# Attention and a squared-ReLU layer in one kernel: first product in pairs of blocks, plainer early blocks, a new written order

## The chip, the cores and the metric

The kernel runs on one core of a Trainium2 chip. The metric is the device time of one execution in microseconds (us). The core has TensorE (PE, matrix products into PSUM), VectorE (DVE), ScalarE (ACT), GpSimd (POOL) and SyncE (SP), each with its own queue of instructions, and DMA engines that POOL and SP feed here.

## The reference

The inputs `q`, `k`, `v` have 4 batches, 8 heads, 768 positions and 64 columns; `w_in` is 512 x 2048 and `w_out` 2048 x 512. All are float32.

```python
scores = q @ k.T / sqrt(64) - slope[h] * dist          # dist: distance back, 96 for the 8 global keys
keep   = (key < 8) | (0 <= query - key < 96)
a      = softmax(where(keep, scores, -1e9))            # over the keys
x      = (a @ v), heads side by side, as 3072 x 512
out    = relu(x @ w_in) ** 2 @ w_out                   # 3072 x 512
```

## The kernel before

**Tiles and blocks.** The 3,072 rows are 24 tiles of 128; tile j = 6b + t is the t-th of batch b. Since a query sees at most 95 keys back and 8 global ones, a tile needs its own keys and those of the tile before it, into which the 8 global ones are copied (`gk` for keys, `gv` for values; every first tile of a batch needs only itself). Two tiles make a block: 12 blocks of 256 rows go through the two layers.

**Attention, per tile.** POOL loads q, k and v with a cast to bf16 (`ld` for the first six tiles, line 330; `load` later, line 334). Queries and keys are transposed: for tiles below `JQK` = 8 by PE through the identity (`tr`, line 528) and a copy out of PSUM (`T`, lines 453 on ACT, 455 on DVE), for the others by one DMA transpose that SP issues (`T`, line 554). `sc` (line 618) makes scores with products of 64 rows. In tiles 0 to 2 the bias, a scaled identity `sid[h]` times a mask, is added by PE ahead of the scores (`bias`, line 597); later tiles multiply the exponential (`exp`, line 684, ACT) by a table `E` (`mul`, line 709, DVE). `pv` (line 767) makes the output and, from a column of ones, the sum, for four heads in a PSUM bank. `norm` (lines 797 and 798, DVE) takes the reciprocal and multiplies, once for each four heads. The tile is transposed again into `xT`: below `JX` = 8 by PE (`trx`, line 835) and a copy, later by DMA (line 859, SP).

**First layer, per block.** In the plain form (`s1`, line 1081) PE makes one step of 256 hidden columns from 8 products of 256 moving columns; `relu` (lines 884, 886) and `sq` (lines 1117, 1119) follow. In the other form (`first_seven`) the block is seen as a 2 x 2 matrix of quarters, here two halves of the 512 input columns and the block's two tiles, and seven products p1 to p7 take the place of eight (line 967). DVE makes sums of `w_in`'s quarters once (`isum`, line 907) and of the block's quarters (`xs`, line 939). The products of one group of steps gather in three PSUM banks, and the order within a group is tied:

```python
p1 = product("p1", "x", (0, 0), (0, 0), True)
u1 = copy(1, "x", p1)
p6 = product("p6", "x", 1, 1, False, [u1])
u2 = copy(2, "x", p6)
p7 = product("p7", "x", 3, 2, False, [u2])
u3 = copy(3, "x", p7)
p4 = product("p4", "x", (1, 1), 3, False, [u3])
```

`u` copies a part result out (453, 455); `c` adds one back and applies the ReLU (line 1011), `q` squares (lines 1031, 1033). Each of these products has 8 matmuls of 128 moving columns, for one tile. Before the change, block 0 and the first half of block 1 are plain; the second half of block 1 (`SEVEN1_PART`) and blocks 2 to 11 (`SEVEN1`) have the seven products.

**Second layer, per block.** All 12 blocks (`SEVEN`) use seven products as well (`s2`, line 1230, matmuls of 256 moving columns), with sums of `w_out` (`wsum`, line 1150) and of the hidden block (`sum`, written to `hsum`, line 1185). `part` and `o` (line 1305) bring the results out, `st` (line 1327) stores through SP.

**What sets the order.** Every step is an operation of a `Plan`. The text constant `ORDER` names all operations in one sequence, with the PSUM banks or buffers that each takes (`:hex digits`) and its engine (`@A` ACT, `@V` DVE). Each engine runs its own operations in that sequence, and semaphores hold it where an operand or a buffer is not ready. POOL and SP follow the sequence too, so a transpose that waits for its load holds the stores behind it. Rings limit how far work can run ahead: 16 buffers, 3 `xT`, 3 hidden blocks (`NHB`), 12 transposed key and query tiles (`NKT`), 10 value tiles (`NV`).

**Head.** Ahead of the planned part, PE runs `NWARM` = 8 products of 512 columns on zeros (line 396), while DVE makes the mask tables, then both identities, then `sid` for the 8 heads (line 414), and ACT fills `E` (line 421).

Of the kernel before, what the change touches and what calls it, by code (L numbers as in the profile page):

```python
# [57 lines left out]
tr.0.0:0 T.0.0@V tr.1.0:1 bias.0.0:23 T.1.0@V ld.q.1 ld.k.1 tr.0.1:4 T.0.1@V ld.q.2 ld.k.2 E0.1 ld.q.3 ld.v.0 ld.k.3  # L58
tr.1.1:5 T.1.1@A ld.v.1 sc.0.0 bias.1.0:6701 exp.0.1.0:0 sc.1.0 tr.0.2:4 exp.0.0.0 gk.1@A T.0.2@V exp.1.0.0:1 tr.1.2:5
T.1.2@V bias.2.0:3264 sc.2.0 exp.1.1.0 exp.1.1.1:3 ld.k.4 exp.1.0.1 ld.q.4 pv.0.1:5 tr.0.3:7 pv.0.0:1 ld.v.2 gk.2@A  # L60
exp.2.1.1:4 exp.2.0.0:5 exp.2.0.1 exp.2.1.0 tr.1.3:0 T.0.3@V T.1.3@V sc.3.0:4730 norm.0.0:0 norm.0.1 pv.1.0:6 tr.1.4:1
ld.q.5 pv.1.1:2 norm.1.0:1 norm.1.1 trx.0:5 exp.3.1.1:6 ld.k.5 gv.1@A ld.v.3 tr.0.4:0 T.1.4@V T.0.4@V xT.0@A:0 gk.3@V
trx.1:6 exp.3.0.1 exp.3.1.0:7 exp.3.0.0 ld.win.1.0 pv.2.0:2 pv.2.1:5 norm.2.0:0 norm.2.1 gv.2@V mul.3.0:8 sc.4.0:1037
exp.4.1.0:9 trx.2:2 ld.win.4.0 xT.1@A exp.4.1.1:a tr.1.5:4 tr.0.5:5 T.1.5@A exp.4.0.0 xT.2@A:1 mul.3.1:b pv.3.0:0
pv.3.1:6 T.0.5@A s1.0.1:7 norm.3.0:1 gk.4@V exp.4.0.1 norm.3.1 gv.3@A s1.0.1#2 trx.3:4 sc.5.0:0126 exp.5.0.1:c
exp.5.1.0:d s1.0.4:5 exp.5.1.1 E0.0 mul.4.0:e xT.3@V ld.v.4 mul.4.1:f ones.6 pv.4.0:3 s1.1.1:4 relu.0.4@V:2 exp.5.0.0
ld.win.3.0 s1.0.3:2 pv.4.1:1 relu.0.1@A:0 sq.0.1@A:0 gv.4@A s1.0.3#2 mul.5.1:1 s1.1.3:6 norm.4.0:0 norm.4.1 ld.win.2.0
# [5 lines left out]
relu.0.6@A:a ld.wout.6 ld.wout.5 ld.wout.4 u.2.1.1@A:e relu.0.7@A:c isum.3.1 s1.0.0#4 h.2.1.p5:4 s1.0.2#3 relu.0.0@A:f
h.1.1.p1:6 h.2.1.p2:7 u.1.1.1@A:0 isum.2.1 h.2.1.p6 u.2.1.2@A:d h.1.1.p2:2 c.1.1.c11:3 xs.2.2 c.2.1.c11:5 sq.0.0@A
s1.0.2#4 isum.2.0 h.1.1.p6 u.1.1.2@A:1 h.2.0.p6 u.2.0.2@A:4 h.2.1.p7 u.2.1.3@A:8 h.1.1.p7 h.2.0.p5:5 relu.0.2@A:6
u.1.1.3@A:2 h.2.0.p7 wsum.0.0 h.1.1.p5:2 u.2.0.3@A:7 c.2.1.c22:b wsum.1.0 sq.0.2@A gate.9 s1.0.5:7 h.2.1.p3 wsum.2.0
c.2.0.c22:f load.6 load.7 c.1.1.c22:0 sq.0.7@A relu.0.5@A:e sq.0.6@A sq.0.5@A load.8 c.2.1.c12:8 sum.0.2:0 sum.0.0
h.1.1.p4 h.2.0.p4 wsum.0.1 s2.1.p1.0:0 T.8 c.2.0.c21@A:6 h.2.0.p3 h.2.1.p4 s2.0.p1.0:7 h.1.1.p3 sum.0.1 s2.0.p2.0:4
q.1.1.c22@A q.1.1.c11@A s2.0.p1.1 q.2.1.c22@A:2 q.2.0.c11@A part.0.p1@A:0 c.1.1.c21@A:c s2.0.p2.1 s2.1.p1.1 wsum.1.1
s2.0.p6.0 s2.0.p6.1 c.1.1.c12:7 tr.1.6:1 tr.0.6:6 part.1.p1@A:1 q.1.1.c21@A s2.1.p2.0:2 q.2.1.c11@A sum.0.3 wsum.2.1  # L80
part.0.p6@A:2 o.0.p2:a c.2.1.c21@A:2 s2.1.p2.1 wsum.3.1 wsum.3.0 T.1.6@V s2.0.p7.0 s2.0.p7.1 gate.12 s2.0.p5.0
q.1.1.c12@A s2.0.p5.1 c.2.0.c12:e load.9 part.0.p7@A:3 q.2.1.c12@A T.0.6@A q.2.0.c22@A o.0.p5:d s2.0.p4.0 s2.0.p4.1
q.2.0.c12@A o.0.p4@A sum.1.0:1 s2.0.p3.0 tr.0.7:3 gate.13 sum.1.1 s2.0.p3.1 o.1.p2:0 o.0.p3 sum.1.2 T.0.7@A tr.1.7:1
sum.2.2:0 sum.1.3 sum.2.0 T.1.7@A q.2.0.c21@A s2.1.p6.0 s2.1.p6.1 q.2.1.c21@A part.1.p6@A:0 sc.6.0:567341 exp.6.1.0:3
load.10 gk.7@A exp.6.0.0 s2.1.p5.0 s2.1.p7.0 s2.1.p7.1 mul.6.0:b exp.7.0.0:9 exp.7.1.0 part.1.p7@A:3 s2.2.p1.0:6
s2.1.p5.1 sum.2.1 exp.7.0.1:1 exp.7.1.1 o.1.p5:c mul.7.0:5 s2.2.p1.1 pv.6.0:5 norm.6.0:0 s2.1.p4.0 s2.1.p4.1 o.1.p4@A
pv.6.1:7 s2.1.p3.0 sc.8.0:3415 exp.8.0.1:7 part.2.p1@A:1 pv.7.0:0 s2.1.p3.1 mul.7.1:8 norm.6.1 T.9 pv.7.1:7 norm.7.0:1
norm.7.1 trx.6:1 exp.8.1.0:4 xT.6@V:0 exp.8.1.1 exp.8.0.0 s2.2.p6.0 s2.2.p6.1 o.1.p3 gate.15 trx.7:0 xT.7@A gk.8@V
# [76 lines left out]
sum.11.1#2 st.8.1 st.9.1 sum.11.2 o.10.p4@A s2.11.p6.0 s2.11.p6.1 st.10.1 o.11.p2:0 st.11.0 sum.11.2#2 part.11.p6@V:1  # L165
s2.10.p3.0 s2.10.p3.1 st.9.0 s2.11.p7.0 s2.11.p7.1 o.10.p3 st.10.0 st.7.1 sum.11.3#2 part.11.p7@V:3 sum.11.3
s2.11.p5.0 s2.11.p5.1 o.11.p5:b s2.11.p4.0 s2.11.p4.1 o.11.p4@V s2.11.p3.0 s2.11.p3.1 st.11.1 st.11.1#2 o.11.p3
st.11.0#2
"""


@with_exitstack
def kernel(
# [743 lines left out]
    def first_seven(blk, groups=(0, 1)):  # L917
# [142 lines left out]
        for g in groups:  # L1060
            group(g)
# [388 lines left out]
```

## Time and profile before

| | |
|---|---|
| median of 3 runs | 197.23 us |
| lowest, highest | 196.97, 197.88 us |
| span of the profiled execution | 195.7 us |
| granted clock of TensorE in it | 1.000 |
| instructions in the span | 6835 |
| DMA | 26.92 MB, mean 138 GB/s |

The profile is of one execution, and the page gives no other time of its own for it than the span, from the first to the last instruction. What the run has beyond that lies around the span. The page lists busy time by engine; a row of the stages gives the busy time of the engines in a stretch; the chain of work that ended last is followed back from the last instruction, each piece to what released it. "PE bank L967" is TensorE writing a PSUM bank at line 967. A matmul's own duration contains the way through the array, so the pace of a row of matmuls is read from a long piece, not from the mean duration of one.

### The profile page before, as it was taken

Reading aid. Unit: us, or ns where it says so; the run is one execution under the profiler, and the core shown is the slowest. Engines: PE = TensorE matmul, PEld = TensorE weight load, DVE = VectorE, ACT = ScalarE, POOL = GpSimd, SP = SyncE. Lnnn points to the kernel's source line nnn. Section 1 sums busy time; section 2 is a strip of 40 time slices with the busy share of each in tenths; the row PEclk is TensorE's granted clock in tenths of the full one; section 3 lists DMA queues with packets and bytes.
Section 4 is the critical chain, followed back from the end, with each engine's and each line's share of the span. In section 5 each row is a group of like instructions: output and inputs, shape, how many; then the busy total and the mean of one; then the engine's idle time right before and its main releaser. Section 6 shows DMA issues by size and latency. Waiting matters only on the chain.

```text
span 195.7 us, 6835 instructions
## 1 busy us (share of the span) xinstructions
PE 188.5 (96%) x2808; PEld 170.5 (87%) x2808; DVE 179.4 (92%) x437; ACT 161.6 (83%) x338; POOL 75.1 (38%) x93
## 2 busy tenths in 40 slices
PE   7986999999999999999999999999999999999993
PEld 3774999999888989989989989989889999999982
DVE  8569989999999999989999999899999899999982
ACT  6699999999989797999899997587987798986600
POOL 8999784775564502650047080119200000000000
PEclk9999999999999999999999999999999999999999
DMA  7999999999999999999949989999947440152026
GB/s 125 149 150 167 179 193 205 205 162 151 155 150 143 99 177 168 119 100 227 139 79 129 138 74 119 209 168 97 147 113 188 85 136 13 20 193 105 0 91 234
DMA packets 111713, 26.92 MB, mean 138 GB/s; under 512 B 103234, under 2 KB 108866, under 8 KB 111682
## 3 DMA queue, kind: packets, MB, share of 16 engines
q0 software_dynamic: 80256, 13.37, 91.9%
q1 hardware_dynamic: 31426, 13.11, 33.4%
q8 instruction: 22, 0.36, 0.7%
q14 instruction: 9, 0.07, 0.1%
HBM read 27.26 MB, written 6.29 MB: 171 GB/s over the span
## 4 chain that ended last, share of the span: by engine, by line
PE 85%; POOL 6%; DMA 5%; DVE 1%; issue 0%; POOLq 0%; DVEq 0%
PE bank L1230 37%; PE bank L967 32%; PE bank L1081 6%; PE bank L618 5%; PE bank L767 5%; POOL qk_first L330 5%; DMA win<-in_moe_w_in_dram 3%; DMA xT<-x 2%; POOL v L330 2%; PE bank L835 1%; PE bank L528 0%; DVE xs L939 0%; DVE buf L886 0%; DVE hsum L1185 0%; DVE early L1305 0%
## 5 line engine op out<-in xcount | busy, mean ns | idle before, releaser
L684 ACT ACTIVATE buf<-bank 128x512 bf16<-128x512 f32 x76 | 41.5, 613 | 2.8 <-PE bank L618 2.7
L1031 ACT ACTIVATE hs<-buf 128x512 bf16<-128x512 f32 x62 | 37.2, 635 | 2.5 <-DVE buf L1011 2.0
L1230 PEld LDWEIGHTS <-hsum 128*128 128x128 bf16 x384 | 35.3, 98 | 4.0
L453 ACT COPY buf<-bank 128x512 f32<-128x512 f32 (+1 forms) x59 | 32.1, 569 | 7.7 <-PE bank L967 6.1
L1230 PE MATMUL bank<-wsum,hsum 128*128 128x256 bf16 x288 | 38.0, 273 | 0.0
L1011 DVE CUSTOM_DVE_ANT_0 buf<-bank,buf 128x512 f32<-128x512 f32 x49 | 33.0, 682 | 0.8 <-ACT buf L453 0.3
L967 PEld LDWEIGHTS <-qk_first 128*128 128x128 bf16 x504 | 31.1, 98 | 1.4 <-issue 0.3
L967 PEld LDWEIGHTS <-win 128*128 128x128 bf16 x504 | 30.8, 98 | 0.9
L334 POOL DMA_DIRECT2D qk<-in_q_dram x18 | 16.0, 889 | 35.3 <-DMA qkT<-qk 30.0
L1230 PEld LDWEIGHTS <-hs 128*128 128x128 bf16 x288 | 26.3, 98 | 2.7
L1230 PE MATMUL bank<-wout,hs 128*128 128x256 bf16 x192 | 27.3, 273 | 0.0
L334 POOL DMA_DIRECT2D v<-in_v_dram x18 | 16.0, 891 | 23.1 <-PE bank L967 13.1
L967 PE MATMUL bank<-xs,qk_first 128*128 128x128 bf16 x336 | 24.6, 219 | 0.2 <-DVE buf L886 0.2
L967 PE MATMUL bank<-xT,win 128*128 128x128 bf16 x336 | 24.6, 219 | 0.0
L709 DVE TENSOR_TENSOR buf<-buf,E 128x1024 bf16<-128x1024 bf16 x32 | 21.5, 683 | 0.5 <-ACT buf L684 0.5
L798 DVE TENSOR_TENSOR x<-bank,rs 128x256 bf16<-128x256 f32 x48 | 20.4, 425 | 1.7
L767 PE MATMUL bank<-v,buf 128*128 128x65 bf16 x312 | 16.1, 193 | 0.9 <-DMA v<-in_v_dram 0.5
L1185 DVE TENSOR_TENSOR hsum<-hs 128x1024 bf16<-128x1024 bf16 (+1 forms) x26 | 16.4, 642 | 0.3
L334 POOL DMA_DIRECT2D qk<-in_k_dram x18 | 16.1, 897 | 0.6 <-DMA wout<-in_moe_w_out_dram 0.4
L767 PEld LDWEIGHTS <-buf 128*128 128x128 bf16 x312 | 13.9, 98 | 1.8 <-DVE buf L709 0.6
L884 ACT ACTIVATE buf<-bank 128x512 f32<-128x512 f32 x23 | 13.7, 607 | 1.0 <-PE bank L967 1.0
L453 ACT COPY part<-bank 128x256 f32<-128x256 f32 x29 | 11.1, 383 | 3.6 <-PE bank L1230 3.6
(92 smaller groups left out, 349.4 us busy)
## 6 DMA issues: line engine op xcount, KB each, us to landing
out_dram<-buf SPq DMA_DIRECT2D x17, 256.0 KB, 2.7
v<-in_v_dram POOLq DMA_DIRECT2D x24, 128.0 KB, 5.4
qk<-in_q_dram POOLq DMA_DIRECT2D x18, 128.0 KB, 5.0
qk<-in_k_dram POOLq DMA_DIRECT2D x18, 128.0 KB, 5.5
wout<-in_moe_w_out_dram POOLq DMA_DIRECT2D x8, 256.0 KB, 9.7
win<-in_moe_w_in_dram POOLq DMA_DIRECT2D x6, 256.0 KB, 7.1
out_dram<-early SPq DMA_DIRECT2D x5, 256.0 KB, 2.7
qk_first<-in_q_dram POOLq DMA_DIRECT2D x5, 128.0 KB, 4.6
```

Of the source, the lines that this page charges most:

```text
L334: nc.gpsimd.dma_start(out=dst, in_=src)
L453: nc.scalar.copy(dst, src)
L684: nc.scalar.activation(out=tiles[tag, j, g][:, odd], in_=tiles.pop(("sc", j, odd, g)).rearrange("p a c -> p (a c)"), func=Act.Exp, scale=s ...
L709: nc.vector.tensor_mul(at, tiles.pop(("esc", j, g)), bias)
L767: nc.tensor.matmul(out=po[:, hi, :], lhsT=tiles["at", j, g][:, odd, at * P : (at + 1) * P], rhs=v_sb[kj][:, h, :], start=(i == 0), stop=(i ...
L798: nc.vector.tensor_tensor(out=x[:, 4 * hf : 4 * hf + 4, :], in0=po[:, :, :D], in1=rs.to_broadcast([P, 4, D]), op=Alu.mult,)
L884: nc.scalar.activation(dst, src, Act.Relu)
L967: nc.tensor.matmul(out=tiles["h", blk, g, bank][:, n], lhsT=left_[:, s, k], rhs=right_[:, k], start=opens and n == 0 and k == 0, stop=k == ...
L1011: nc.vector._custom_dve(TENSOR_ADD_SAT, out=hr, in0=src, in1=tiles.pop(("u", blk, g, i)), s0=float("inf"), s1=0.0,)
L1031: nc.scalar.activation(hs, hr, Act.Square)
L1185: nc.vector.tensor_tensor(out=t[:, i, h], in0=t[:, a, h] if isinstance(a, int) else half_a(blk, *a)[:, h], in1=t[:, b, h] if isinstance(b, ...
L1230: nc.tensor.matmul(out=tiles["acc", blk, bank][:, cols], lhsT=left_[:, s], rhs=right_[:, cols], start=first and s == 0, stop=s == NSTEP - ...
```

## The change

- **Pairs.** For blocks (4, 5), (6, 7), (8, 9), (10, 11) the quarters of the first layer's seven products are the two blocks rather than a block's two tiles: a product has 4 matmuls of 256 moving columns, a group spans two steps instead of four (so four groups for a pair, not two for each block), and the squares go to the hidden tiles of two blocks. A pair takes both `xs` buffers; DVE makes its four sums singly. The rings of `xT` and of hidden blocks grow from 3 to 4.
- **Early blocks.** Block 1's second half goes back to `s1`; block 0's second layer goes back to the plain form, 32 matmuls of 512 columns (line 1393 after). That code was there before, unused.
- **Transposes.** `JQK` and `JX` go from 8 to 6: tiles 6 and 7 are transposed by DMA, at both ends of the attention.
- **Normalisation.** `pv` takes two neighbouring banks, and one reciprocal of 8 and one multiplication of 512 columns follow for the tile.
- **Head.** 3 warm-up products instead of 8; `sid` is made by ACT rather than DVE, ahead of `E`; the first identity is made first and the second last; the bias products no longer wait for the transposes, and those of tile 1 open PE's order.
- **Order.** `ORDER` is written anew throughout. Key and value rings shrink to 9.

```diff
-tr.0.0:0 T.0.0@V tr.1.0:1 bias.0.0:23 T.1.0@V ld.q.1 ld.k.1 tr.0.1:4 T.0.1@V ld.q.2 ld.k.2 E0.1 ld.q.3 ld.v.0 ld.k.3
+bias.1.0:0123 ld.q.1 bias.0.0:45 tr.0.0:6 ld.k.1 T.0.0@A tr.1.0:7 T.1.0@A ld.k.2 tr.1.1:6 T.1.1 tr.0.1:7 T.0.1 sc.0.0
...
-    JQK, JX = 8, 8
+    JQK, JX = 6, 6
...
-    NQ, NKT, NV = 3, 2 * TPB, 10
+    NQ, NKT, NV = 3, 9, 9
...
-    banks = [ps.tile([P, 4 * P], FP32, name=f"bank_{i}", tag=f"bank_{i}") for i in range(NBANK)]
+    bank_all = ps.tile([P, NBANK, 4 * P], FP32, name="bank", tag="bank")
+    banks = [bank_all[:, i] for i in range(NBANK)]
...
-    NHB = 3
-    SEVEN = set(range(NBLK))
+    WHOLE = True
+    PAIRS = ((4, 5), (6, 7), (8, 9), (10, 11))
+    NHB = 4
+    NXT = 4
+    SEVEN = set(range(1, NBLK))
     SEVEN1 = set(range(2, NBLK))
-    SEVEN1_PART = {(1, 1)}
+    SEVEN1_PART = set()
...
-    NWARM = 8
+    NWARM = 3
...
+    nc.vector.tensor_scalar(ident32, pbi[:, 0, :], 0.0, None, op0=Alu.is_equal)
+    for h in range(H):
+        nc.scalar.activation(sid[h], ident32, Act.Copy, scale=float(slopes[h] / scale))
...
-    for h in range(H):
-
-        nc.vector.scalar_tensor_tensor(
-            out=sid[h], in0=ident32, scalar=float(slopes[h] / scale), in1=ident32,
-            op0=Alu.mult, op1=Alu.mult,
-        )
+    nc.vector.tensor_scalar(ident, pbi[:, 0, :], 0.0, None, op0=Alu.is_equal)
...
-                    lambda e, gs=gs, f=emit_bias: f(e, gs), deps=[tr],
+                    lambda e, gs=gs, f=emit_bias: f(e, gs), deps=[],
...
+            def emit_whole(e, j=j):
+                tiles["x", j] = lent("x")
+                x, po = tiles["x", j], tiles.pop(("po", j))
+                rs = work.tile([P, 2, 4, 1], FP32, name="rs", tag="rs")
+                nc.vector.reciprocal(rs, po[:, :, :, D : D + 1])
+                nc.vector.tensor_tensor(
+                    out=x.rearrange("p (b a) c -> p b a c", b=2),
+                    in0=po[:, :, :, :D],
+                    in1=rs.to_broadcast([P, 2, 4, D]),
+                    op=Alu.mult,
+                )
...
-    def first_seven(blk, groups=(0, 1)):
-        husers = hs_users.setdefault(blk, [])
-        tusers = []
+    def first_seven(blk, groups=(0, 1), mate=None):
+        blks = (blk, blk) if mate is None else (blk, mate)
+        wide = mate is not None
+        GRP = 2 if wide else 4
+        W = 2 * P if wide else P
...
         def part_x(kh, sub):
-            return tiles["xT", blk][:, 2 * kh : 2 * kh + 2, sub * P : (sub + 1) * P]
+            t = tiles["xT", blks[sub]][:, 2 * kh : 2 * kh + 2]
+            return t if wide else t[:, :, sub * P : (sub + 1) * P]
...
-                    hs = hidden(blk)[:, steps, c, sub * P : (sub + 1) * P]
+                    hs = hidden(dst)[:, steps, c]
+                    if not wide:
+                        hs = hs[:, :, sub * P : (sub + 1) * P]
...
-        for g in groups:
+        for g in range(4) if wide else groups:
             group(g)
...
-            if s == 0:
-                first_seven(blk)
+            if s == 0 and blk not in [z[0] for z in PAIRS]:
+                pair = [z for z in PAIRS if z[1] == blk]
+                if pair:
+                    first_seven(pair[0][0], mate=blk)
+                else:
+                    first_seven(blk)
```

Two spots of the new order are spoken of below. The end of PE's part ahead of the first `w_in` product, and the opening of the first pair (words of other engines stand between):

```
... pv.3.0:23 pv.3.1 norm.3:0 exp.4.1.1 trx.2:1 sc.5.0:6450 exp.5.0.0:5 xT.2@A:1 exp.5.1.0 exp.5.1.1:4 ld.win.1.0 s1.0.1:7
... h.4.2.p1:7 u.4.0.1:9 xs.4.0:01 xs.4.2 h.4.0.p6 h.4.1.p6 u.4.2.1:3 c.4.0.c11:5 u.4.3.1:9 q.4.0.c11 h.4.2.p6
```

More of the change, by code (lines that the diff above doesn't have):

```diff
@@ L63 @@
[L63 to L67, printed above, removed]
@@ L73 @@
[L73 to L77, printed above, removed]
@@ L78 @@
[L78 to L87, printed above, removed]
@@ L303 @@
     }
+    xs_all = const([P, 2, 4 * 2 * P], BF16, "xs")
+    buffers["xs"] = [xs_all[:, i].rearrange("p (z k c) -> p z k c", z=4, k=2) for i in range(2)]
     buffers["buf"] = [early[:, i] for i in range(3)] + buffers["buf"]
@@ L754 @@
         xusers = []
+        both = [[], []]
         for hf in range(2):
@@ L779 @@
                 deps.append(glob.get(("v", j - 1)))
+            if WHOLE:
+                users = both[hf]
+                deps += pvs
             p_ = plan.op(
@@ L782 @@
                 key=base + 2 + 2 * hf,
-                takes=(*G, [users]),
+                takes=(*G, [users] if not WHOLE else both) if hf == 0 or not WHOLE else None,
             )
+            if WHOLE and hf == 0:
+                p_["adj"] = 2
             mul_users[g].append(p_)
```

295 lines of the change are left out of this document (160 added, 135 removed).

## The prediction

> **What bounds the kernel now.** I read the page's shares first, then the stages, then the chain that ended last.
>
> ```profile
> span 195.7 us, 6835 instructions
> PE 188.5 (96%) x2808; PEld 170.5 (87%) x2808; DVE 179.4 (92%) x437; ACT 161.6 (83%) x338; POOL 75.1 (38%) x93
> ...
> 5.00:10.00 5.00, 4.75 (x67) 3.93 (x66) 2.89 (x7) 3.12 (x9) 5.00 (x6) 1.00 2.35 150
> 10.00:15.00 5.00, 4.15 (x86) 3.28 (x84) 3.41 (x13) 4.96 (x12) 5.00 (x7) 1.00 2.34 150
> 15.00:20.00 5.00, 3.59 (x68) 2.75 (x69) 4.79 (x14) 4.87 (x11) 5.00 (x8) 1.00 1.81 169
> 20.00:25.00 5.00, 5.00 (x86) 4.58 (x83) 4.86 (x16) 4.67 (x10) 3.64 (x5) 1.00 1.87 179
> 60.00:80.00 20.00, 20.00 (x326) 18.26 (x324) 19.47 (x48) 17.05 (x37) 6.35 (x8) 1.00 1.34 139
> 180.00:190.00 10.00, 10.00 (x110) 9.13 (x108) 9.33 (x22) 4.24 (x10) 0.00 (x0) 1.00 0.15 52
> ```
>
> The stage rows read: stretch, length, then busy us of TensorE (PE), its weight loads, VectorE (DVE), ScalarE (ACT), GpSimd (POOL), granted clock, DMA share, GB/s. Between 5 and 20 us PE leaves 0.25 + 0.85 + 1.41 = 2.5 us open while POOL is full and, from 10 us, ACT too. From 20 us PE is full in every row. Busy is not the same as fast, so the chain decides (start, length, what):
>
> ```profile
> 13.60 6.01 DMA win<-in_moe_w_in_dram
> ...
> 19.66 1.07 PE bank L1081 x16
> ...
> 20.95 0.55 PE bank L618 x16
> ...
> 35.40 3.13 PE bank L967 x56
> ...
> 182.77 9.64 PE bank L1230 x88
> ```
>
> The chain is POOL issuing loads, the landing of the first slice of `w_in` at 19.66 us, and then PE alone. A first-layer product of 128 columns costs 3.13/56 = 55.9 ns, a second-layer one of 256 columns 9.64/88 = 109.5 ns: both hold their pace over long rows, with weight loads under them. So there are two bounds: the landing at 19.66 us, and the TensorE work that the order leaves for after it. A tail follows:
>
> ```profile
> 188.45 3.90 SPq L1327 DMA_DIRECT2D out_dram<-buf  x5
> ...
> 192.44 0.42 DVE L1305 TENSOR_TENSOR early<-bank,part 128x256 f32<-128x256 f32 x1 [0.45 <-PE bank L1230]
> 192.89 0.33 SPq L1327 DMA_DIRECT2D out_dram<-early  x1
> ```
>
> From the last sum at 192.44 to 195.7 is 3.3 us of sum, store and landing. SP issues five stores in the 3.90 us ahead of it; the new order again leaves a dozen stores of late blocks to the last 13 us and ends with two of half a row, so I keep the tail as it is. Outside the span lie 197.23 − 195.7 = 1.5 us between the profiled execution and the median of the runs; I add the change to the median.
>
> **The parts, on TensorE.** Counting both programs' instructions: first-layer products of blocks 4 to 11 go from 896 of 128 columns to 448 of 256 columns. That is 896 × 55.9 = 50.1 us against 448 × 109.5 = 49.1 us: −1.0 us. No row has a 256-column product with these operands, but the second layer's row has the same shape; if the weight loads hid worse than there, the end is 896 × 55.9, that is nothing gained.
>
> The Trainium skill, TensorE: Matmul & The Clock Gate, Back-to-back issue gap, gives a sustained 81 ns for a product of 128 columns with its weight load. By it, 896 × 81 − 49.1 = 23.5 us would go; the row of 56 products at 55.9 ns disagrees, and I leave that out.
>
> The second half of block 1 becomes plain: 56 × 55.9 = 3.1 us out, 32 × 109.5 = 3.5 us in, +0.4. The second layer of block 0 becomes plain: 56 × 109.5 = 6.1 us out, 32 products of 512 columns in. 512 columns appear only in the warm-up, at the start, where PE has not come to its pace:
>
> ```profile
> L396 PE MATMUL bank<-early 128*128 128x512 bf16 x8 | 3.6, 631 | 1.2 <-DVE early L385 1.2
> ```
>
> They take 3.6/8 = 0.45 us each there; twice the 256-column price is 0.219. The second is from the saturated stage, where these will run: 7.0 us, +0.9 (the warm-up price would make it 14.4 us, +8.3, and is far away in time). Tiles 6 and 7 lose 16 input and 8 output transposes of 128 columns: 24 × 55.9 = −1.3. Sum: −1.0 + 0.4 + 0.9 − 1.3 = **−1.0 us** of PE work.
>
> **The start.** Both orders place the first `w_in` load as the fifteenth load on POOL, so it should land at 19.66 again. Ahead of the first product with it, the new order has the same transposes, biases and scores as the old, plus the scores of tile 5, which now stand at 20.95 behind it: −0.55, and with the change into and out of 64-row products some 0.05 more, **−0.6 us**. This holds if ACT lets those scores start by then, since they take the bank of tile 4's third exponential:
>
> ```profile
> 2.03 0.20 ACT L393 ACTIVATE junk<-early 128x1 f32<-128x1 bf16 x1
> 3.32 2.56 ACT L421 ACTIVATE E<-pb 128x256 bf16<-128x256 bf16 x8 [1.09 <-DVE pb L410]
> 7.96 1.09 ACT L684 ACTIVATE early<-bank 128x512 bf16<-128x512 f32 x2
> ...
> L453 ACT COPY qkT<-bank 128x512 bf16<-128x512 bf16 x6 | 3.5, 604 | 1.6 <-PE bank L528 1.6
> ```
>
> ACT now makes the eight scaled identities. They begin at 2.2 us and at the price of the eight bias exponentials (2.6 us, wider, so an upper end; nothing is the lower) end by 4.8; the bias exponentials end by 7.4, two copies of tile 0 by 8.6. Then come 17 exponentials. Two take 1.09, so one more adds 0.5: 8.5 us, with three copies and a small one 2 us: 19.1 us. ACT is in time by 0.6 us, without any idle. If it idles 1 us, the scores are 0.4 late. The bias of tile 1 moves to a time in which PE only warms up; it saves latency, hidden by the landing.
>
> **VectorE and ScalarE.** One normalisation a tile:
>
> ```profile
> L798 DVE TENSOR_TENSOR x<-bank,rs 128x256 bf16<-128x256 f32 x48 | 20.4, 425 | 1.7
> L797 DVE RECIPROCAL rs<-bank 128x4 f32<-128x4 f32 x48 | 8.7, 180 | 0.6
> L455 DVE CAST qkT<-bank 128x512 bf16<-128x512 f32 x2 | 1.3, 686 | 0.6 <-PE bank L528 0.6
> L1031 ACT ACTIVATE hs<-buf 128x512 bf16<-128x512 f32 x62 | 37.2, 635 | 2.5 <-DVE buf L1011 2.0
> ```
>
> Per tile 2 × (0.425 + 0.180) = 1.21 us becomes about 0.686 + 0.18 = 0.87: 24 × 0.34 = 8 us off DVE. Blocks 0 and 1 need fewer part sums, and ACT squares 8 tiles fewer, 8 × 0.635 = 5 us. Neither engine is on the chain from 20 us on, so nothing of this enters the sum; it is the cover for the rival below. The wider pieces leave the number of evictions per block alone; their tiles span two blocks, for which the rings of hidden tiles and of transposed outputs grow to four. The smaller rings of keys (9) and values (9) only touch loads that POOL issues late with time to spare (38% busy).
>
> Transposes of tiles 6 and 7 go to SP's queue:
>
> ```profile
> qkT<-qk SPq DMA_TRANSPOSE x16, 5.2
> xT<-x SPq DMA_TRANSPOSE x16, 2.7
> ...
> 123.03 4.44 DMA xT<-x
> ```
>
> Inputs are loaded some 15 us of PE work ahead, so 5.2 us is hidden. The output transpose of tile 6 stands between its normalisation and the first product of block 3, with about 3.7 us of PE words between: 2.7 is hidden, 4.44 (the worst on the chain) is 0.7 late.
>
> **Sum:** −1.0 − 0.6 = −1.6 us. Span 194.1, median **195.6**. The kernel resolves about 0.5%, or 1 us: faster is below 196.2, slower above 198.2.
>
> **Rivals.** *Hand-overs in the wide chain (the slower side).* In a group p1, copy, p6, copy, p7, copy, p4 share a bank, so PE waits if its order has nothing between a copy and the next product.
>
> ```profile
> L453 ACT COPY buf<-bank 128x512 f32<-128x512 f32 x51 | 29.3, 600 | 6.2 <-PE bank L967 6.1
> ...
> PE bank L967 <- DVE buf L886: 0.2, 1, 0.2
> ```
>
> In the written order a product follows the word of its copy, with no PE word between, at 6 places before and 11 after (four of them in block 4); a second-layer product so follows its hidden-sum at 1 place before and 5 after, mostly in the last 10 us. A full wait is 0.6 us: 11 × 0.6 + 5 × 0.68 = 10 us if all bite, none if words mean nothing. Against it: of the six before only 0.2 us shows as a wait; DVE and ACT get lighter. For it: the stage of 60 to 80 us has DVE at 97%. At a third, 3.3 us: 198.9. It decides from 2.6 us of waits on, four or five full ones. Chance 0.20, and 0.10 for a milder form of 1 to 2 us, 196.6 to 197.6.
>
> *The clock comes late.* Eight warm-up products (3.6 us) become three, with a gap until the masks are ready. At 0.45 against 0.219 us the start runs at about half pace. One more such stretch of 3.4 us costs up to 3.4 us of PE time against the 2.5 us open before 20 us: +0.9, 196.5. Chance 0.08. The Trainium skill, the same page's Part 1: The HAM clock gate, speaks against this part: it asks some 3.4 us of sustained activity before full clock. The warm-up row agrees (full pace after 3.6 us); what three do no run shows.
>
> *The transposes by DMA hold block 3.* SP's order puts tile 8's transpose, which waits for tile 8's load behind seven `w_out` loads, ahead of tile 6's output. If that load is late, PE stands: 2.8 us or more decides it, 198.5 with a wait of 2.9. The load should issue at about 40 us, the need is at about 57. Chance 0.05.
>
> *Better than the sum.* A shorter tail and the last small waits gone: at most 1 us more, 194.5. Chance 0.04. That the change does not do what it says has no room: the matmul count drops from 2,808 to 2,283.
>
> **How the numbers follow.** Forecast 0.53 (194.8 to 196.2), better 0.04: faster 0.57. Mild waits 0.10 and the clock 0.08: same 0.18. Waits 0.20 and block 3 0.05: slower 0.25. The range leaves out the worst waits and little below: 194.1 to 199.1.
>
> **What would show it.** Right: 448 products of 256 columns at 109 to 110 ns; the first product with `w_in` at about 19.7 us, behind the scores of tile 5; PE full from 20 us; the last product near 190.6 us. Wrong: PE waiting on ACT or DVE in blocks 4 to 11, or on sums in the last 10 us; a first product after 20.5 us; the warm-up pace lasting past 8 us; a first-layer product above 112 ns.

## The result and the profile after

The changed kernel takes **220.21 us** (median of 4 runs, 218.85 to 221.18) against 197.10 us of the kernel before beside it: a ratio of 1.1157, 95% interval 1.1109 to 1.1206. The forecast was 195.6 us in a range of 194.1 to 199.1. It was wrong in size and in sign. The profiled execution has a span of 218.7 us; as before, 1.5 us lie between span and median. Medians here are over all runs of a kernel, while ratios and intervals leave out runs more than 1.5% above the kernel's fastest.

From the page: span, busy time by engine, granted clock in 40 slices, the chain that ended last.

```profile
span 218.7 us, 5789 instructions
...
PE 193.1 (88%) x2281; PEld 162.8 (74%) x2283; DVE 172.7 (79%) x371; ACT 156.0 (71%) x326; POOL 75.3 (34%) x93
...
PEclk9999999995899999799999999999969999999999
...
PE 53%; DMA 29%; POOL 6%; DVE 5%; ACT 2%; issue 2%; SPq 0%; DVEq 0%; POOLq 0%; ACTq 0%
```

The page has 527 matmul records fewer (the program has 525 matmuls fewer), yet PE is busy 4.6 us longer (193.1 against 188.5), and four slices have a lower clock. PE stands for 25.6 us of the span against 7.2 before, 18.4 us more; the two together are the 23.0 us that the span grew. A DMA is what is waited for in 29% of the chain. The stages, columns as in the prediction, show where:

```profile
43.90:51.00 7.10, 0.74 (x10) 0.23 (x8) 4.54 (x9) 1.37 (x3) 3.16 (x4) 0.90 1.59 172
51.00:56.50 5.50, 5.27 (x27) 2.52 (x29) 1.30 (x2) 4.35 (x9) 2.63 (x3) 0.51 2.43 155
...
87.00:90.10 3.10, 0.67 (x8) 0.36 (x5) 0.91 (x3) 0.91 (x2) 0.48 (x1) 1.00 2.37 151
90.10:94.00 3.90, 3.90 (x21) 2.79 (x22) 3.87 (x8) 1.95 (x4) 0.67 (x1) 0.56 1.67 181
...
151.00:158.00 7.00, 2.97 (x37) 2.39 (x36) 3.57 (x7) 2.52 (x5) 0.00 (x0) 1.00 1.31 199
158.00:161.50 3.50, 3.50 (x34) 2.66 (x29) 2.70 (x6) 2.34 (x6) 0.00 (x0) 0.61 0.00 0
161.50:219.00 57.50, 53.76 (x552) 47.52 (x549) 47.22 (x96) 32.12 (x67) 0.00 (x0) 0.99 0.21 70
```

Three times the same picture: a stretch in which PE stands (6.4, 2.4 and 4.0 us idle), and behind it 3.5 to 5.5 us at a clock of 0.51 to 0.61. The pace lost in these three is 5.5 × 0.49 + 3.9 × 0.44 + 3.5 × 0.39 = 5.8 us. The last row, with the loads over (POOL does nothing) and the last pair in it, has PE busy for 53.76 of 57.5 us, and the other 3.7 are the tail behind its last product: nothing is lost there. The chain names what PE stood for (start, length, what):

```profile
30.32 7.46 DMA qk<-in_k_dram
...
37.79 13.17 DMA qkT<-qk
...
51.01 1.03 PE bank L608 x16
...
52.81 3.62 PE bank L1393 x8
...
57.33 0.43 PE bank L1393 x2
...
64.31 5.64 DMA xT<-x
...
83.35 5.71 DMA xT<-x
...
123.07 1.75 PE bank L1006 x16
...
149.10 6.27 DMA out_dram<-buf
```

The transpose of tile 7's queries and keys is issued at 37.79 us and lands 13.17 us later, and the scores of tile 7 (L608) start at that moment. At 64.31 us it is the output transpose of tile 7. At 83.35 us it is the output transpose of tile 11, for which the first pair's sums wait; at 149.10 a store of block 5, whose buffer a multiplication wants next. In PE's own order the two stands before the scores of tiles 6 and 7 are these (start, length, what, in brackets the idle time before it):

```profile
46.39 0.40 PE L608 MATMUL bank<-qkT 64*128 64x128 bf16 x8 [2.14 <-DMA qkT<-qk]
51.01 0.29 PE L608 MATMUL bank<-qkT 64*128 64x128 bf16 x2 [4.23 <-DMA qkT<-qk]
```

The waits by engine (total, times, longest):

```profile
POOL qk L328 <- DMA qkT<-qk: 20.8, 6, 7.8
...
PEld L608 <- DMA qkT<-qk: 11.4, 5, 4.4
...
PE bank L608 <- DMA qkT<-qk: 7.8, 4, 4.2
...
DVE xs L975 <- DMA xT<-x: 4.8, 2, 2.7
...
DVE buf L699 <- DMA out_dram<-buf: 3.2, 1, 3.2
```

And POOL while the transposes of tiles 6 and 7 are in flight (issued at 34.03 and 37.79 us):

```profile
32.56 2.38 POOL L324 DMA_DIRECT2D wout<-in_moe_w_out_dram  x3 [0.20 <-issue]
35.50 0.70 POOL L324 DMA_DIRECT2D wout<-in_moe_w_out_dram  x1 [0.56 <-DMA wout<-in_moe_w_out_dram]
36.39 1.55 POOL L324 DMA_DIRECT2D wout<-in_moe_w_out_dram  x2 [0.19 <-issue]
```

The loads of `w_out`, and behind them of tile 8, run beside these two transposes. Before the change the last load of `w_out` was issued at 31.27 us and the first transposing DMA at 48.91.

### The profile page after: what moved, and what is told of

Read it like the earlier page. It is cut to its first block, busy times and chain, and to the rows that moved or that the text cites. A ratio compares the mean times of both kernels' runs of the same rounds, so it can differ in the third digit from the quotient of the medians.

```text
span 218.7 us, 5789 instructions
## 1 busy us (share of the span) xinstructions
PE 193.1 (88%) x2281; PEld 162.8 (74%) x2283; DVE 172.7 (79%) x371; ACT 156.0 (71%) x326; POOL 75.3 (34%) x93
## 4 chain that ended last, share of the span: by engine, by line
PE 53%; DMA 29%; POOL 6%; DVE 5%; ACT 2%; issue 2%; SPq 0%; DVEq 0%; POOLq 0%; ACTq 0%
PE bank L1266 25%; PE bank L1006 19%; DMA qkT<-qk 9%; DMA win<-in_moe_w_in_dram 7%; DMA xT<-x 5%; DMA out_dram<-buf 4%; POOL qk_first L324 4%; DMA qk<-in_k_dram 3%; PE bank L1393 3%; PE bank L761 3%; PE bank L608 3%; POOL v L324 2%; DVE buf L1051 1%; ACT buf L674 1%; DVE x L796 1%
## 5 line engine op out<-in xcount | busy, mean ns | idle before, releaser
L674 ACT ACTIVATE buf<-bank 128x512 bf16<-128x512 f32 x64 | 35.6, 608 | 10.2 <-PE bank L608 9.6
L443 ACT COPY buf<-bank 128x512 f32<-128x512 f32 (+1 forms) x48 | 25.5, 550 | 16.2 <-PE bank L1266 4.7
L328 POOL DMA_DIRECT2D v<-in_v_dram x18 | 16.1, 892 | 46.3 <-PE bank L1006 13.2
L1006 PE MATMUL bank<-xs,qk_first 128*128 128x256 bf16 (+1 forms) x192 | 24.3, 264 | 2.4 <-DVE xs L975 2.4
L1006 PEld LDWEIGHTS <-win 128*128 128x128 bf16 x288 | 24.2, 98 | 2.9 <-issue 0.2
L1051 DVE CUSTOM_DVE_ANT_0 buf<-bank,buf 128x512 f32<-128x512 f32 x36 | 24.3, 684 | 1.9 <-PE bank L1006 1.8
L608 PE MATMUL bank<-qkT 64*128 64x128 bf16 x192 | 12.9, 222 | 13.2 <-DMA qkT<-qk 7.8
L608 PEld LDWEIGHTS <-qkT 64*128 64x128 bf16 x352 | 10.5, 96 | 17.2 <-DMA qkT<-qk 11.4
L1006 PE MATMUL bank<-xT,win 128*128 128x256 bf16 (+1 forms) x192 | 22.5, 255 | 0.1
L796 DVE TENSOR_TENSOR x<-bank,rs 128x512 bf16<-128x512 f32 x24 | 16.6, 692 | 2.9 <-DMA xT<-x 2.0
L1341 DVE TENSOR_TENSOR buf<-bank,part 128x256 f32<-128x256 f32 x31 | 13.0, 420 | 4.6 <-PE bank L1266 4.1
L674 ACT ACTIVATE early<-bank 128x512 bf16<-128x512 f32 x24 | 13.6, 608 | 4.0 <-PE bank L608 2.9
```

Source lines behind the costliest of these rows:

```text
L328: nc.gpsimd.dma_start(out=dst, in_=src)
L443: nc.scalar.copy(dst, src)
L608: nc.tensor.matmul(out=tiles["sc", j, odd, g][:, at, :], lhsT=left[j - 1][half, pair, :] if kt else qkT[j % NKT][half, 1, pair, :], rhs=qk ...
L674: nc.scalar.activation(out=tiles[tag, j, g][:, odd], in_=tiles.pop(("sc", j, odd, g)).rearrange("p a c -> p (a c)"), func=Act.Exp, scale=s ...
L796: nc.vector.tensor_tensor(out=x.rearrange("p (b a) c -> p b a c", b=2), in0=po[:, :, :, :D], in1=rs.to_broadcast([P, 2, 4, D]), op=Alu.mult,)
L1006: nc.tensor.matmul(out=tiles["h", blk, g, bank][:, n], lhsT=left_[:, s, k], rhs=right_[:, k], start=opens and n == 0 and k == 0, stop=k == ...
```

## The experiments

Each run's own kernel before took 197.3 to 198.0 us. Medians are in us; an interval is that of the ratio to the kernel before.

### Tiles 6 and 7

**Their queries and keys back on TensorE** (outputs still by DMA):

```diff
-    JQK, JX = 6, 6
+    JQK, JX = 8, 6
-... T.6 ... T.7 ...
+... tr.0.6 T.0.6 tr.1.6 T.1.6@A h.2.0.p7 ... tr.0.7 T.0.7 tr.1.7 T.1.7@A h.2.1.p3 ...
```

> The changed kernel with the queries and keys of tiles 6 and 7 transposed by TensorE again, about 8 us of PE order ahead of their scores. Theory (TensorE waits for DMA transposes that land 12 to 13 us after their issue): the wait of 2.1 + 4.2 us at 44 to 51 us goes, and with it the stretch at half clock behind it (about 2.4 us); 0.9 us of PE work comes back; 220.2 becomes about 212 (210 to 214). Rival (the wait only hides another one: the wide chains or the engines beside TensorE): 218 or more.

Measured: **209.54** (1.0561, 1.0483 to 1.0638), 10.7 us less than the change and a little below the theory's range, though PE has 0.9 us more to do. Its stages of 40 to 60 us:

```profile
40.00:50.00 10.00, 9.89 (x114) 7.01 (x113) 9.32 (x17) 9.62 (x20) 6.72 (x8) 1.00 1.76 184
50.00:60.00 10.00, 8.80 (x109) 6.23 (x107) 8.56 (x19) 6.90 (x16) 3.44 (x4) 1.00 1.70 175
```

The two long waits and the low clock are gone there. This part makes about half of the loss.

**PE kept busy in the wait**, 16 products on data of no use between the scores of tiles 6 and 7:

```diff
+                    if j == 6 and at:
+                        for i in range(16):
+                            nc.tensor.matmul(out=psum(at), lhsT=ident, rhs=..., start=True, stop=True)
                     f(e, gs, at)
```

> The changed kernel with 16 useless products of 512 columns between the scores of tile 6 and those of tile 7, written to a bank that the next scores overwrite, so that TensorE is busy for 3.5 of the 4.2 us in which it waits for tile 7's transpose. Theory (waits of over some 3 us cost half the clock afterwards): the granted clock from 51 to 56.5 us is 1.0 instead of 0.51, and 2.3 us come back: about 218. Rival (the clock falls for another reason): clock as before there and 220 or more.

Measured: 220.58 (217.62 to 225.03; 1.1038, 1.0930 to 1.1147), no gain that is clear of the scatter, as the interval overlaps that of the change. But the clock did change, and the chain tells why it was worth little:

```profile
50.00:60.00 10.00, 9.95 (x77) 5.64 (x77) 5.30 (x11) 5.56 (x12) 2.65 (x4) 1.00 2.23 167
```

```profile
62.53 7.36 DMA xT<-x
```

From 50 to 60 us PE got 77 matmuls done at full clock, some nine of them of no use, against 55 at a mean of 0.68. Then it stood from 67.2 to 71.0 us, behind the output transpose of tile 7. That was issued at 62.53 us, 1.8 us sooner than in the change (64.31), but took 7.36 us rather than 5.64, so both landed at 69.9. The half clock was real and cost next to nothing in that stage: the chain of DMAs was behind it.

**`w_out` loaded first, as before; the transposes stay DMAs:**

```diff
-... load.6 ... ld.wout.0 ... load.7 ld.wout.1 ... ld.wout.2 ld.wout.3 ... ld.wout.5 ... ld.wout.7 ld.wout.4 ... ld.wout.6 ...
+... ld.wout.0 ld.wout.1 ld.wout.2 ld.wout.3 ld.wout.5 ld.wout.7 ld.wout.4 ld.wout.6 load.6 ... load.7 ...
```

> The changed kernel with its eight loads of w_out moved ahead of the loads of tiles 6 and 7, as they stood in the kernel before; the transposes by DMA stay. Theory (a transposing DMA is slow while the loads of w_out are on the DMA engines): the transposes of tiles 6 and 7 are issued some 6 us later, near 40 and 44 us, but land in 5 to 7 us instead of 12.3 and 13.2; the scores of tiles 6 and 7 wait 4 to 8 us in all instead of 13; 213 to 217 us. Rival (12 to 13 us is what these transposes take in this order, whoever loads): the waits grow by the 6 us of later loads, 223 to 228 us.

Measured: 219.61 (217.24 to 221.12; 1.0953 to 1.1076), neither of the two; by the intervals it takes some 1% less than the change. The time from issue to landing of the transposes of queries and keys (least, median, most), for the changed kernel from 30 to 60 us (tiles 6 to 8) and for this one from 30 to 62 us (also three):

```profile
DMA to landing us min/median/max: 8.4/12.3/13.2
```

```profile
DMA to landing us min/median/max: 4.3/6.1/7.7
```

So the landing depends on what else is on the DMA engines, as the theory had it. Its times were not right: the transposes were issued at 44.1 and 46.6 us rather than 40 and 44, and what the landing gained the issue lost. PE stood 7.7 us for the scores of tile 6, against 2.14 + 4.23 for both tiles in the change. The Trainium skill, DMA: Bandwidth & Descriptors, SWDGE vs HWDGE vs iDMA, says that the DMAs of GpSimd and of SyncE go to the same engines, which take turns between the queues. These two rows agree as to the sharing, and show nothing of the turns.

**Queries and keys loaded ahead of values, with one buffer more:**

```diff
-    NQ, NKT, NV = 3, 9, 9
+    NQ, NKT, NV = 4, 8, 9
-                load_v(j)
                 load_part(0, j)
                 load_part(1, j)
+                load_v(j)
```

> The changed kernel with GpSimd issuing queries and keys of a tile before its values, so that they do not stand behind the wait for a free value buffer, and a ring of raw query and key tiles one longer (the ring of transposed ones goes from 9 to 8 for the room). Theory (later waits come from loads and transposes issued too late): the first wait at 44 to 51 us stays, those at 65, 111 and 151 us shrink: 220 becomes 212 to 217. Rival (the transposes are slow because the DMA engines are shared, however early they are issued, or buffers in PSUM and SBUF set the pace): 219 to 222.

Measured: 214.95 (1.0756 to 1.0908), 5.3 us less, within the theory's range. The gain came late: the output transpose of tile 19 is issued at 139.56 us against 140.24 in the change, that of tile 20 at 157.84 against 163.25. Between the two lies the store that takes 6.27 us to land in the change, and it lands sooner here:

```profile
148.02 3.24 DMA out_dram<-buf
```

Then both edits in one kernel:

> The changed kernel with both edits that helped alone: queries and keys of tiles 6 and 7 transposed by TensorE, and the loads issued queries and keys first with one buffer more. Alone they gave 10.7 us and 5.3 us. Theory (two separate causes: the late transposes of tiles 6 and 7, and late loads for the tiles behind them): near 204 us, 203 to 206, the first wait for transposed inputs after tile 8 under 1 us each. Rival (one cause: the late loads only hurt through the transposes of tiles 6 and 7, which are gone here): 209 to 210 us, as with the first edit alone.

Measured: 209.73 (1.0566 to 1.0661), the same as the first edit alone. The rival's figure came, but not by its reason: the loads alone had gained at the store, not at the scores of tiles 6 and 7. With both edits PE stands 1.2 us instead of 2.9 from 135 to 165 us, but 2.9 instead of 1.3 from 40 to 60, where half a clock follows again. The wait moved; why is open.

**That part alone, on the kernel before:**

```diff
-    JQK, JX = 8, 8
+    JQK, JX = 6, 8
-... T.8 ... tr.1.6 tr.0.6 ... T.1.6 ... T.0.6 ... tr.0.7 ... T.0.7 tr.1.7 ... T.1.7 ...
+... T.6 T.7 T.8 ...
```

> The kernel before with one part of the change alone: queries and keys of tiles 6 and 7 transposed by DMA, issued directly ahead of that of tile 8; all else as before. There the loads of w_out are over by 31 us, the loads of these tiles are issued at 32.5 to 39.8 us, and their scores come at 51.6 us. Theory (the transposes are dear only for where the change put them): issued near 43 and 46 us, landed in 5 to 7 us, at 48 to 53 us; TensorE has 0.66 us less work and waits up to 2 us; 196.5 to 199.5 us. Rival (transposing inputs of early tiles by DMA is dear in itself): 203 to 208 us.

Measured: 202.84 (1.0280, 1.0212 to 1.0349), just short of the rival's 203 and far from the theory: 4.9 us dearer than the kernel before also in an order that was not written for it. Its waits from 40 to 65 us:

```profile
POOL qk L333 <- DMA qkT<-qk: 7.6, 1, 7.6
...
PE bank L617 <- DMA qkT<-qk: 3.8, 2, 3.3
```

A buffer for loaded queries and keys is held here until the transposing DMA has landed, and POOL's next load waits 7.6 us for it. With a fourth buffer:

```diff
-    NQ, NKT, NV = 3, 2 * TPB, 10
+    NQ, NKT, NV = 4, 2 * TPB, 10
-                load_v(j)
                 load_part(0, j)
                 load_part(1, j)
+                load_v(j)
```

> The kernel before with queries and keys of tiles 6 and 7 transposed by DMA (alone it took 202.8 us), four buffers for loaded queries and keys instead of three, and each tile's queries and keys issued ahead of its values. Theory (a buffer that TensorE's transposes free at once is held until the DMA has landed, GpSimd's next load waits for it, 7.6 us in the profile of that run, and the transposes of tiles 8 and 9 come late): the wait on GpSimd and the 3.3 us at tile 9's scores are gone; 197 to 199.5 us. Rival (the landing times alone decide, not the buffers): 201.5 to 203 us.

Measured: 204.40 (1.0276 to 1.0372), no gain, and somewhat above the rival's range too; the wait at tile 9 went and one of 3.1 us at the scores of tile 7 took its place. And with the loads of tiles 6 and 7 ahead of the last three of `w_out`:

```diff
-... ld.wout.6 ld.wout.5 ld.wout.4 ... load.6 load.7 ...
+... load.6 load.7 ld.wout.6 ld.wout.5 ld.wout.4 ...
```

> The kernel before with queries and keys of tiles 6 and 7 transposed by DMA and four buffers (204.4 us with the loads where they were), and the loads of tiles 6 and 7 moved ahead of the last three loads of w_out, so that they are issued some 2.5 us earlier. Theory (in that order the transposes lack 4 us between issue and use, 4.3 us of waits at 50 to 55 us): half to all of that wait goes, 200 to 202 us; below 197 us only if nothing else becomes late. Rival (a transposing DMA with loads of w_out beside it takes 12 us, as in the changed kernel): 203 to 207 us.

Measured: 204.08 (1.0302 to 1.0381), in the rival's range. Transposes from 38 to 60 us, and what PE waited for from 38 to 50 us:

```profile
DMA to landing us min/median/max: 8.2/9.5/9.9
```

```profile
PE bank L1229 <- DMA wout<-in_moe_w_out_dram: 4.0, 1, 4.0
```

Issued sooner, the transposes took longer (6.1 to 9.3 us in the run before it, with a median of 8.2), and now PE waited for `w_out`, in the second layer: what one transfer gained the other lost.

### Pairs

**Each matmul of 256 columns as two of 128**, the pairs otherwise as they are:

```diff
+                            for z in range(2 if wide else 1):
+                                cols = slice(z * P, z * P + P)
                                 nc.tensor.matmul(
-                                out=tiles["h", blk, g, bank][:, n], lhsT=left_[:, s, k], rhs=right_[:, k],
+                                out=tiles["h", blk, g, bank][:, n, cols], lhsT=left_[:, s, k], rhs=right_[:, k, cols],
```

> The changed kernel with each 256-column matmul of the paired products split into two of 128 columns, same tiles, banks and order: 448 matmuls become 896. Theory (the DMA waits): slower by 0 to 1.5 us against the changed kernel, 220 to 222, for 1.0 us more PE work of which part falls into waits. Rival (the wide matmuls themselves, their weight loads or evictions, cost the time): several us faster, 215 or less.

Measured: 223.34 (1.1128 to 1.1320), 3.1 us more than the change, beyond the theory's 222 and on the other side from the rival's 215. The wide products are not what cost the time.

**Outputs of tiles 6 and 7 on TensorE too**, on the run with their inputs there, so that nothing of that part is left:

```diff
-    JQK, JX = 8, 6
+    JQK, JX = 8, 8
-... xT.6 h.3.1.p1 ... h.3.0.p1 ... xT.7 xs.3.0 ...
+... trx.6 xT.6@A h.3.1.p1 ... trx.7 xT.7@A h.3.0.p1 ... xs.3.0 ...
```

> The changed kernel with inputs and outputs of tiles 6 and 7 transposed by TensorE, so with no part of that edit left (the run with the inputs alone took 209.5 us). It adds 0.9 us of TensorE work and takes two 5 us transposes off the chain of block 3 and off SP's queue. Theory (what is left over the kernel before is mostly waits for transposing DMAs): 206 to 208 us. Rival (the outputs' transposes lay hidden): 209.5 to 211 us.

Measured: 211.93 (209.13 to 217.38; too scattered for an interval). No gain over 209.54, as the rival had it, as far as the scatter allows. It is the base of the next runs. **The pairs undone on it:**

```diff
-    PAIRS = ((4, 5), (6, 7), (8, 9), (10, 11))
+    PAIRS = ()
-... h.4.1.p2 ... h.4.1.p1 ... h.4.3.p1 ... h.4.0.p1 ...
+... h.4.0.p2 ... h.4.0.p1 ... h.4.1.p1 ... h.5.0.p1 ...
```

> The run above, and the four pairs undone in the same written order: the two first groups of a pair become block b, the two others block b+1, in products of 128 columns; 15 of the 1190 steps, sums and the products of the second layer among them, move back because a block's parts are now ready at other points. 448 products of 109 ns become 896 of 56 ns, 1 us more of TensorE. Theory (a pair opens only when all four of its tiles are transposed, and this costs some 3 us at the first pair and half a clock behind it): 2 to 4 us less than the run above. Rival (the opening is paid for elsewhere anyway): 1 us more than the run above, or up to 3 more where the moved steps wait.

Measured: 234.15 (1.1801 to 1.1892). Far outside both; the written order is too closely fitted to pairs for this to say what pairs cost. **Outputs of tiles 8 to 11 on TensorE:**

```diff
-    JQK, JX = 8, 8
+    JQK, JX = 8, 12
-... xT.8 ... xT.9 ... xT.10 ... xT.11 ...
+... trx.8 xT.8@A ... trx.9 xT.9@A ... trx.10 xT.10@A ... trx.11 xT.11@A ...
```

> The run with inputs and outputs of tiles 6 and 7 on TensorE, and the outputs of tiles 8 to 11 as well, so that the first pair's inputs come by no DMA; 32 transposes more, 1.8 us of TensorE, and four copies on ScalarE. Theory (the first pair waits for the transposing DMA of its last tile, 5.7 us behind its issue): the wait near 80 us is gone and the clock stays full behind it; 1 to 3 us less than the run with tiles 6 and 7 alone. Rival (the wait is for the tile's own scores, which come late): 1 to 2 us more than that run.

Measured: 214.38 (1.0769 to 1.0893), no gain, and the rival's side. The base, then this run:

```profile
80.00:100.00 20.00, 16.92 (x198) 14.45 (x196) 16.41 (x34) 16.20 (x35) 9.36 (x11) 1.00 1.96 167
100.00:120.00 20.00, 18.48 (x247) 16.14 (x246) 18.16 (x39) 17.54 (x38) 5.53 (x8) 1.00 1.46 156
```

```profile
80.00:100.00 20.00, 20.00 (x238) 17.27 (x237) 19.10 (x37) 19.46 (x42) 10.80 (x13) 1.00 1.44 145
100.00:120.00 20.00, 17.03 (x227) 14.85 (x220) 16.74 (x38) 16.39 (x37) 4.71 (x6) 1.00 1.62 154
```

The wait at the opening of the first pair is gone, 3.1 us, but from 100 to 120 us PE stands 3.0 us against 1.5, and with 32 transposes more PE is busy 2.2 us longer over the whole run (192.0 against 189.8). So the wait was the transposing DMA's, as the theory had it, and taking it away was no gain.

### SP's queue

**Every store directly behind the last step that fills its buffer**, on the kernel with loads ahead and TensorE's input transposes (209.73):

```diff
-... o.4.p4 ... o.4.p3 ... st.5.0 ... st.5.1 ... T.21 ... st.4.1 ... st.4.0 ...
+... o.4.p4 st.4.1 ... o.4.p3 st.4.0 ... st.5.0 ... st.5.1 ... T.21 ...
```

> The same as the run with both edits, and each store of the output moved in the written order to directly behind the last step that fills its buffer (the stores of block 4 had stood 190 and 430 steps later, those of blocks 0, 1, 6 and 7 also late). Theory (two multiplications of late blocks waited for a store that was issued only then, 4 us of TensorE and half a clock behind it): 4 to 5 us less than the run with both edits, near 200 us, and no wait for a store in the chain near 140 to 155 us. Rival (that wait is slack that the next wait takes up, or the stores now stand ahead of transposes on SP's queue and push those back): within 1 us of the run with both edits, or up to 3 us more.

Measured: **228.95** (1.1447 to 1.1622), 19 us more; the rival in kind, at six times its price. SP's waits ahead of stores for DVE's results, in the base, and for DVE's and ACT's here:

```profile
SPq L1364 <- DVE buf L1342: 42.4, 9, 19.2
```

```profile
SPq L1364 <- DVE buf L1342: 53.3, 14, 20.6
...
SPq L1364 <- ACT buf L444: 13.6, 6, 4.0
```

A store that stands in SP's queue before its data is there holds the transposes behind it: block 1's two stores go out at 67.8 and 72.9 us, and right behind them, at 68.3 and 73.4, the transposes of tile 7's output and tile 10's inputs, which the base issues in the stretch from 56.3 to 58.9. **Only the late queue**, with the stores of blocks 4 and 6 where their data has long been there, and tile 21's transpose directly behind tile 20's; on the run with tiles 6 and 7 on TensorE, then with the loads ahead, then with the outputs of tiles 8 to 11 as well, and on the change itself:

```diff
-... T.20 ... st.5.0 ... T.21 ... st.4.1 ... st.7.0 ... st.6.1 ... st.6.0 ... st.4.0 ...
+... T.20 T.21 ... st.4.0 st.4.1 st.5.0 ... st.6.0 st.6.1 st.7.0 ...
```

> The run with inputs and outputs of tiles 6 and 7 on TensorE (211.9 us, profiled span 209.2), and on SP's queue the stores of blocks 4 and 6 moved to directly ahead of the first stores of blocks 5 and 7, where their data has long been there, and the transpose of tile 21's inputs to directly behind that of tile 20. Theory (the 3.7 us wait near 145 to 150 us is an effect of the queue's order): that wait is gone and the multiplication that waited for a store too; 206 to 208.5 us. Rival (another wait takes its place): within 1 us of that run.

> The run above with four buffers for loaded queries and keys and each tile's queries and keys issued ahead of its values. Theory (the buffers hold back the loads of tiles 10 and 11 by 8 us, and these are late at 50 to 70 us): 1.5 to 3 us less than the run above. Rival (as on the run with TensorE's input transposes alone, no effect): within 1 us.

> The run above with the outputs of tiles 8 to 11 transposed by TensorE. Theory (the first pair's wait for the last transposing DMA, 3.2 us in the profile without this, is a loss of its own once later waits are gone): 1 to 2 us less than the run above, TensorE's 1.8 us paid. Rival (the order behind it is paced by something else): 1 to 2 us more.

> The changed kernel with the same two edits of SP's queue and nothing else: the transposes by DMA of tiles 6 and 7 stay. Theory (the 4.4 us at 150 to 155 us, a multiplication that waits for a store of block 4, are a cause apart from the transposes, with half a clock behind): 214 to 216 us. Rival (the wait is taken up elsewhere): 219 to 221 us.

Measured: 214.02, 212.65, 213.80 and 220.28 (intervals 1.0766 to 1.0906, 1.0681 to 1.0799, 1.0734 to 1.0868, 1.1063 to 1.1199). No theory held. The third and the fourth run came out as their rivals had it, the first two as neither. The reading behind them was wrong too: the store at 149.10 us in the chain of the change is the second of block 5, not one of block 4. It stands behind the transpose of tile 22, as it does in these runs, and the chain of the first has it still:

```profile
141.29 7.18 DMA out_dram<-buf
```

So these four show that moving the stores of blocks 4 and 6 and tile 21's transpose gains nothing here. What block 5's store costs by itself was not tried: the run with 228.95 moved it with others.

### The traffic

**Loads from tile 9 on cut to two heads of eight**, on the run with tiles 6 and 7 on TensorE (211.93):

```diff
+        hh = slice(0, 2 if j > 8 else H)
-        swdge(("v", j), v_sb[j][:, :, :D], src_rows(v, j).rearrange("h p d -> p h d"), 0.87)
+        swdge(("v", j), v_sb[j][:, hh, :D], src_rows(v, j)[hh].rearrange("h p d -> p h d"), 0.87)
...
-            src_rows((q, k)[n], j).rearrange("h p d -> p h d"), 0.85,
+            src_rows((q, k)[n], j)[: 2 if j > 8 else H].rearrange("h p d -> p h d"), 0.85,
```

> The run with inputs and outputs of tiles 6 and 7 on TensorE (211.9 us, profiled span 209.2), with the loads of queries, keys and values from tile 9 on cut to two heads of eight; the other six heads keep what an earlier tile left in the buffer. Number and order of all instructions stay. Theory (landing times under the traffic of the loads make the waits that are left): the waits of TensorE between 75 and 160 us fall from 10 us to under 5; 203 to 206 us. Rival (the written order asks for transposed tiles sooner than even an undisturbed chain of load, transpose, scores, normalisation and transpose can give them): 208 to 212 us.

Measured: **202.90** (1.0241 to 1.0319), with the same order of instructions 9.0 us below the base's median and 6.2 below its fastest run; a little better than the theory's range. Stages of the base, then of this run:

```profile
75.00:100.00 25.00, 21.60 (x250) 18.63 (x247) 20.78 (x44) 20.21 (x43) 11.18 (x14) 1.00 2.01 163
120.00:160.00 40.00, 37.62 (x426) 31.98 (x424) 34.26 (x68) 32.73 (x69) 6.96 (x8) 0.96 0.80 90
```

```profile
75.00:100.00 25.00, 23.97 (x289) 20.78 (x287) 23.36 (x48) 22.74 (x49) 10.53 (x15) 1.00 0.93 117
120.00:160.00 40.00, 39.17 (x461) 34.17 (x460) 37.40 (x76) 32.81 (x69) 2.11 (x3) 1.00 0.38 70
```

PE's idle time in these two stretches falls from 5.8 to 1.9 us, and the clock stays full. Landing of all output transposes, base and this run:

```profile
DMA to landing us min/median/max: 2.4/4.7/8.7
```

```profile
DMA to landing us min/median/max: 2.4/3.1/4.7
```

The order mostly runs when DMAs land sooner; under the full loads they do not. The run does not separate two things: the cut loads themselves land sooner too (3.1 us in the median for queries, against 6.3), which can bring transposes forward as well.

## Why the prediction was wrong

- **The step that failed:** "Inputs are loaded some 15 us of PE work ahead, so 5.2 us is hidden." Both halves of it failed. The 15 us hold only from the issue of the loads: those of tile 6's and tile 7's keys are issued at 26.39 and 30.32 us and take some 7.5 us to land. So the transposes are issued at 34.03 and 37.79, and PE is ready for the scores at 44.25 and 46.8, only 10.2 and 9.0 us later. The 5.2 was the median of transposes that the kernel before issued from 48.91 us on; with the `w_out` loads in flight, where no row of before showed a transposing DMA, the new ones land in 12.3 and 13.2 us. The inputs' part of this edit, entered at −0.9 us of PE work (16 of the 24 transposes), made 10.7 us of the loss. Larger prices were at hand in the profile before: 6.01 us for a load on the quoted chain, and for the loads of `w_out`, the neighbours here, a median of 9.7:

```profile
wout<-in_moe_w_out_dram POOLq DMA_DIRECT2D x8, 256.0 KB, 9.7
```

- **The same step, later on:** for the output transposes it took "2.7 is hidden, 4.44 (the worst on the chain) is 0.7 late". Tile 6's took 2.42 and was hidden, but on the chain of the changed kernel tile 7's takes 5.64 and tile 11's 5.71. Of the 12 to 14 us that are left with tiles 6 and 7 on TensorE, some 6 to 9 go when the loads are cut; a range, because that base scattered.
- **Not in the sum at all:** that a wait brings half a clock behind it. What was said of the 512-column products, that "the warm-up price … is far away in time", did not hold. That price came back: 3.62/8 = 0.45 us each at 52.81 us, 0.43/2 = 0.215 at 57.33. The Trainium skill, TensorE: Matmul & The Clock Gate, Part 1: The HAM clock gate, has the clock halved after about 3.4 us without work. The first and the third low row agree (stands of 4.23 and 3.4 us just before); before the second PE stood only 2.4 us of 3.1.
- **Right, and beside the point:** the paired product costs 1.75/16 = 109 ns, and the 512-column one 0.215 against the 0.219 taken; DVE lost 6.7 us of work (8 forecast), ACT 5.6 (5). In the run with cut loads, at full clock throughout, PE is busy for 189.6 us; the forecast with the 1.3 us of transposes back gives 188.8, so the terms of PE work were right to about 1 us. The first `w_in` product did come behind the scores of tile 5, but landed 0.5 us later than taken, and the 0.6 us of the start did not show:

```profile
20.15 0.62 PE L1127 MATMUL bank<-xT,win 128*128 128x128 bf16 x8 [0.16 <-DMA win<-in_moe_w_in_dram]
```

- **The rivals:** hand-overs in the wide chain (0.20) do not lead the waits: PE's first-layer products stood 0.8 us for them. The clock did not come late (the eight first transposes take 1.04 us, against 1.54 before), it was lost later. The nearest was the one at 0.05, transposes held on SP's queue: tile 8's load did issue near 40 us as priced (its keys at 41.11), but the price was one wait of 2.9 us, not a chain of late transposes. (A wait of 2.6 us, not 2.8, already passes its bound of 198.2, and the last product would be near 190.8, not 190.6; neither changes the forecast.)
- **What stays open:** 5.6 us between the run with small loads and the kernel before, the price of pairs by themselves (the run that undid them undid the order), how much of the gain with cut loads is the transposes' and how much the loads' own, and whether an order with more lead would make the pairs pay. No kernel tried beat the kernel before.

## What to carry to other kernels

Price a DMA by what is in flight where it will run, not by its median where it runs now, and if no row shows one there, take the landing times of its neighbours as the bound. Count its lead from the landing of what it reads, not from the issue. Moving 0.9 us of work off a full engine onto DMA engines that are busy too pays only if the lead is longer than the landing under load, and here it held the source buffer for as long. In this hand-written order a single wait taken away was seldom a gain: filling PE's wait, a fourth buffer in the order before, the first pair's outputs on TensorE and the moved stores and transposes each ended less than 2 us below their base, or above it. Loading queries and keys ahead gave 5.3 us alone and nothing more beside the inputs of tiles 6 and 7, which counted for 10.7 us; cutting the loads counted for 6 to 9.

## What was not expected of the hardware

The transposes of queries and keys, all of one shape, landed in anything from 3.0 to 13.2 us within one run, that of the changed kernel:

```profile
DMA to landing us min/median/max: 3.0/5.0/13.2
```

A stand of PE of 2.4 us was followed by 3.9 us at a clock of 0.56 (87 to 94 us), though a longer one elsewhere (from 80 us on in the run with inputs and outputs of tiles 6 and 7 on TensorE, 3.1 us idle) left it at 1.00.
